# Exchanging row maxima by maximum operations, and moving the row sums of a slot behind its block of feed-forward work

## The chip, the cores and the metric

The kernel runs on one core of one Trainium2 chip. The metric is the device time of one execution in microseconds (us). The core has five engines that run their own instruction streams in order and meet through semaphores: TensorE (PE in the profile; PEld is its weight load), VectorE (DVE), ScalarE (ACT), GpSimd (POOL) and SyncE (SP, which here only issues transfers). SBUF is the on-chip memory with 128 partitions; PSUM is where TensorE writes.

## The reference

Attention with a threshold, then a gated feed-forward block. B = 8 batches, H = 8 heads, S = 576 rows of D = 64; the feed-forward block takes 4608 tokens of 512 through a width of 1536. All is float32.

```python
scale = 1.0 / np.sqrt(q.shape[-1])
scores = scale * np.matmul(q, k.transpose(0, 1, 3, 2))
thresh = np.max(scores, axis=-1, keepdims=True) - tau
scores = np.where(scores >= thresh, scores, -1000000000.0)
scores = scores - np.max(scores, axis=-1, keepdims=True)
attn = np.exp(scores)
attn = attn / (np.sum(attn, axis=-1, keepdims=True) + 1e-09)
attn_out = np.matmul(attn, v)
x = attn_out.transpose(0, 2, 1, 3).reshape(B * S, H * D)
g = x @ w_gate
silu = g * (1.0 / (1.0 + np.exp(-g)))
out = (silu * (x @ w_val)) @ w_out
```

For every row of scores, so, a maximum is needed before anything else, and a sum after the masking.

## The kernel before

Two heads are handled together: a segment is one pair of heads of one batch (32 pairs). A segment consists of tiles of 128 rows of queries; a slot is the work on one tile, and behind the scores of each slot come two portions of the feed-forward block of tokens that are already through attention. `fill(part)` emits such a portion. The first batch is handled tile by tile with whole rows in a lane (20 slots). From the second batch on, segments are *halved* (28 segments of 5 slots, 140 in all): a row of 576 scores lies half in one group of 32 partitions and half in the neighbouring group. So the maximum and the sum of a row are each made in two halves, and neighbouring groups must exchange them. The function `meet` does that: column 0 of a small tile holds a group's own half, and column 1 gets the neighbour's. Four copies do it, one for each group of 32 partitions.

```python
def meet(x, m, copy):
    for g in range(NG):                      # NG = 4 groups of G = 32 partitions
        o = g ^ 1
        copy(x[g * G:(g + 1) * G, 0:m, 1:2], x[o * G:(o + 1) * G, 0:m, 0:1])
```

The scores of one tile are a generator; the main loop advances it between portions of the block (m is 4 halves of rows per lane, 2 in the last tile of a segment):

```python
def scores(seg, t):
    # ... score tiles in PSUM (ps_s: 2 buffers of 2 banks; a full tile takes both) and their matmuls (L266) ...
    if halved:
        # ...
        for x, tile_ in enumerate(pss):
            nc.vector.tensor_reduce(out=mx[:, 2 * x:2 * x + 2, 0], in_=tile_[:, :, 0:SH],
                                    axis=AX.X, op=ALU.max, negate=True)               # L286
        meet(mx, m, nc.vector.tensor_copy)                                            # L244
        nc.vector.tensor_reduce(out=nm[:, 0:m], in_=mx[:, 0:m, :], axis=AX.X, op=ALU.min)   # L289
    # ... the case of whole rows ...
    if halved:
        nc.scalar.activation(th[:, 0:m], nm[:, 0:m], AF.Identity, bias=cut, scale=-1.0)     # L298
    for x in range(m):
        # ...
        nc.scalar.activation(ps[x], scs[x], AF.Exp, bias=nm[:, x:x + 1])              # L302
    yield                                                                             # 1
    turn(1)                                  # turns p of an earlier tile in 32x32 blocks (L334)
    for x in range(m):                       # masking, with the sum of each half row
        nc.vector.scalar_tensor_tensor(out=ps[x], in0=scs[x], scalar=th[:, x:x + 1], in1=ps[x],
                                       op0=ALU.is_ge, op1=ALU.mult, accum_out=sm[:, x, 0:1])   # L306
    tot = stp.tile([P, 4], F32, name="tot")
    if halved:
        meet(sm, m, nc.scalar.copy)                                                   # L244
        yield                                                                         # 2
        nc.vector.tensor_reduce(out=tot[:, 0:m], in_=sm[:, 0:m, :], axis=AX.X, op=ALU.add)  # L312
    # ... else: the sum alone ...
    nc.vector.reciprocal(out=ri[:, 0:m], in_=tot[:, 0:m])                             # L315
    if not halved:
        yield                                                                         # 2
    for x in range(m):
        if halved and not split:             # split: weights are still being joined
            nc.gpsimd.tensor_scalar(out=ps[x], in0=ps[x], scalar1=ri[:, x:x + 1], ...)      # L320
        else:
            nc.scalar.activation(ps[x], ps[x], AF.Copy, scale=ri[:, x:x + 1])         # L322
    # ... p goes on a list, to be turned two slots later ...
    yield                                                                             # 3
```

The block's part in a portion is a gate product (`pg`, 8 or 16 matmuls) that ScalarE copies out of PSUM, a value product (`pv`) that VectorE multiplies with it, or output matmuls (`po`):

```python
def gate(j, cs, f, hts, gts):
    # ...
    ps = rows_of_products(j, cs, f, 0, "pg")                                          # L443
    nc.scalar.copy(gts[f // per][:, f % per:f % per + GR, :], ps)                     # L457

def value(j, cs, f, hts, gts):
    # ...
    ps = rows_of_products(j, cs, f, 1, "pv")                                          # L443
    nc.vector.tensor_tensor(out=hts[f // 2][:, :, 0:n], in0=gts[...], in1=ps, op=ALU.mult)  # L463

def sigmoids():                              # once enough gates have gathered
    for _, gt, own in unsig:
        nc.scalar.activation(gt, gt, AF.Sigmoid)                                      # L472
        for x, ht in enumerate(own):
            nc.gpsimd.tensor_tensor(out=ht, in0=ht, in1=gt[:, 2 * x:2 * x + 2, :], op=ALU.mult)  # L474
```

The main loop, cut to the order of a slot:

```python
for n, seg in enumerate(segs):
    for x, t in enumerate(seg["tiles"]):
        go = scores(seg, t)
        next(go)                             # to yield 1
        # ... transposes and products of whole-row tiles, loads, a piece of weights split ...
        next(go)                             # to yield 2
        if more:
            join_weights()                   # 4 VectorE, 2 GpSimd operations, in the first stage only
        fill(part)                           # first part
        next(go)                             # to yield 3
        if len(unsig) >= SIG:
            sigmoids()
        fill(part)                           # second part
        if attends and n > 2 * NP:
            next(products)                   # p times v (xa, L401), copies to xall (L412, L420)
            next(products)
        # ... loads, and VectorE's transposes of the next segment's q and k ...
```

Of the kernel before, what the change touches and what calls it, by code (L numbers as in the profile page):

```python
# [13 lines left out]
ALU = mybir.AluOpType  # L14
AX = mybir.AxisListType
# [3 lines left out]
def kernel(  # L19
# [28 lines left out]
    nc = tc.nc  # L48
# [6 lines left out]
    G = 32  # L55
# [25 lines left out]
    op = ctx.enter_context(tc.tile_pool(name="op", bufs=1))  # L81
# [112 lines left out]
    def need(n):  # L194
        while len(joined) < n:
            fetch_weights(2)
            if not split:
                split_weights()
            join_weights()
            split_weights()  # L200
# [39 lines left out]
    def meet(x, m, copy):  # L240

        for g in range(NG):
            o = g ^ 1
            copy(x[g * G:(g + 1) * G, 0:m, 1:2], x[o * G:(o + 1) * G, 0:m, 0:1])  # L244

    def scores(seg, t):
        qT, kT, tiles, halved = seg["qT"], seg["kT"], seg["tiles"], seg["halved"]
        if halved and "p" not in seg:
            seg["p"] = ptp.tile([P, 2 * NT + 1, S], F32, name="p")
        q0 = t * P - seg["q0"]  # L250
        heads = [slice(h * D, (h + 1) * D) for h in range(2)]
        if t < NT:
            pss = [ps_s.tile([P, 2, 512], F32, name="sc") for _ in range(2)]
            at = [tiles.index(t), len(tiles) + tiles.index(t)]
        else:
            pss = [ps_s.tile([P, 2, 512], F32, name="sc")]
            at = [tiles.index(t)]
        if halved:
            put = [(pss[h], u, h, q0 + u * D) for u in range(2) for h in range(2)] if t < NT else \
                [(pss[0], h, h, q0) for h in range(2)]  # L260
            for x in range(0, len(put), 2):
                for g in range(NG):
                    a, c = divmod(g, 2)
                    for ps, u, h, col in put[x:x + 2]:
                        hs = heads[h]
                        nc.tensor.matmul(ps[g * G:(g + 1) * G, u, 0:SH], qT[hs, col + a * G:col + (a + 1) * G],  # L266
                                         kT[hs, c * SH:(c + 1) * SH], start=True, stop=True)
        elif t < NT:
            for h, hs in enumerate(heads):
                for n in range(2):  # L270
                    nc.tensor.matmul(pss[h][:, n, 0:SH], qT[hs, q0:q0 + P], kT[hs, n * SH:(n + 1) * SH],
                                     start=True, stop=True)
        else:
            for n, h in ((0, 0), (1, 1), (1, 0), (0, 1)):
                hs = heads[h]
                nc.tensor.matmul(pss[0][hs, n, 0:SH], qT[hs, q0:q0 + D], kT[hs, n * SH:(n + 1) * SH],
                                 start=True, stop=True)
        mx, nm, th, ri = (stp.tile([P, 4, 2] if x == "mx" else [P, 4], F32, name=x) for x in ("mx", "nm", "th", "ri"))
        sm = sums[0]
        sums.rotate(1)  # L280
        if halved:
            m = 2 * len(at)
            scs = [ps[:, u, 0:SH] for ps in pss for u in range(2)]
            ps = [seg["p"][:, x, u * SH:(u + 1) * SH] for x in at for u in range(2)]
            for x, tile_ in enumerate(pss):
                nc.vector.tensor_reduce(out=mx[:, 2 * x:2 * x + 2, 0], in_=tile_[:, :, 0:SH], axis=AX.X, op=ALU.max,  # L286
                                        negate=True)
            meet(mx, m, nc.vector.tensor_copy)
            nc.vector.tensor_reduce(out=nm[:, 0:m], in_=mx[:, 0:m, :], axis=AX.X, op=ALU.min)  # L289
        else:  # L290
            m = len(at)
            scs = [ps[:, :, 0:SH] for ps in pss]
            ps = [pbufs[0][:, x, :].rearrange("p (n s) -> p n s", n=2) for x in range(m)]
            pbufs.rotate(1)
            for x in range(m):
                nc.vector.tensor_reduce(out=nm[:, x:x + 1], in_=scs[x], axis=AX.XY, op=ALU.max, negate=True)
# [4 lines that stand above are left out]
                nc.scalar.activation(th[:, x:x + 1], nm[:, x:x + 1], AF.Identity, bias=cut, scale=-1.0)  # L301
            nc.scalar.activation(ps[x], scs[x], AF.Exp, bias=nm[:, x:x + 1])  # L302
        yield
        turn(1)
        for x in range(m):
            nc.vector.scalar_tensor_tensor(out=ps[x], in0=scs[x], scalar=th[:, x:x + 1], in1=ps[x],  # L306
                                           op0=ALU.is_ge, op1=ALU.mult, accum_out=sm[:, x, 0:1])
        tot = stp.tile([P, 4], F32, name="tot")
        if halved:
            meet(sm, m, nc.scalar.copy)  # L310
            yield
            nc.vector.tensor_reduce(out=tot[:, 0:m], in_=sm[:, 0:m, :], axis=AX.X, op=ALU.add)  # L312
        else:
            nc.vector.tensor_reduce(out=tot[:, 0:m], in_=sm[:, 0:m, 0:3:2], axis=AX.X, op=ALU.add)
        nc.vector.reciprocal(out=ri[:, 0:m], in_=tot[:, 0:m])  # L315
        if not halved:
            yield
        for x in range(m):
            if halved and not split:
                nc.gpsimd.tensor_scalar(out=ps[x], in0=ps[x], scalar1=ri[:, x:x + 1], scalar2=None, op0=ALU.mult)  # L320
# [3 lines that stand above are left out]
            unturned.append([seg["p"][:, x, :] for x in at])  # L324
        else:
            unflipped.append((seg, t, [p.rearrange("p n s -> p (n s)") for p in ps]))
        yield

    unturned = deque()

    def turn(keep):
        while len(unturned) > keep:
            for p in unturned.popleft():
                nc.vector.transpose(out=p, in_=p)  # L334
# [223 lines left out]
    def fill(n):  # L558

        credit[0] += n  # L560
        while credit[0] > 0:
            c = next(pieces)
            left[0] -= c
            credit[0] = credit[0] - c if c else 0
            if not c:
                return 0
        return 1
# [53 lines left out]
    def fetch_qk(i):  # L621
        if i < NPAIR and i not in raws and i not in kept:
            raws[i] = load_qk(i)
# [23 lines left out]
    def give(n):  # L647
        for u in segs[n]["gives"]:
            ready.append(u)
            left[0] += cost(u)  # L650
        gains[n] = (gains[n][0], 0)
# [9 lines left out]
    for n, seg in enumerate(segs):  # L661
        if NP <= n < 2 * NP:
            seg["v"] = segs[seg["i"]]["v"]
        for x, t in enumerate(seg["tiles"]):
            go = scores(seg, t)
            next(go)
            attends = prev is not None and x == 1
            products = iter(())
            attend_tile()
            flip()  # L670
            if n == NP and x == 0:
                attend_tile()
                give(n - 1)
            if n == 2 * NP and x == 1:
                give(n - 1)
            if attends and n > 2 * NP:
                if prev["i"] % NP == 0:
                    need(NCC * DFF // FW + DM // ne * DFF // FW)
                    start_batch(prev["i"] // NP)
                products = attend(prev)  # L680
            part = pace(n, x) / 2
            more = len(split)
            if n or x:
                split_weights()
                fetch_weights(2)
            if x == 0 and n >= NP:
                fetch_qk(seg["i"] + 1)
            next(go)
            if more:
                join_weights()  # L690
            fill(part)
            next(go)
            if len(unsig) >= SIG:
                sigmoids()
            fill(part)
            if attends and n > 2 * NP:
                next(products)
                next(products)
                give(n - 1)
            if attends and seg["halved"]:  # L700
                load_v(seg)
            if x == 0 and 0 < n < NP:
                load_v(seg)
            if x == len(seg["tiles"]) - 2 and n + 1 < len(segs):
                prepare(segs[n + 1])
                if n < NP:
                    fetch_qk(segs[n + 1]["i"] + 1)
        prev = seg
# [39 lines left out]
```

## Time and profile before

| what | value |
|---|---|
| time, median of 3 runs | 1701.67 us (1696.55 to 1704.74) |
| span of the profiled execution | 1702.9 us |
| mean granted TensorE clock | 0.97 |
| VectorE copies of maxima (L244) | 560, 189.8 us, 339 ns each |
| ScalarE copies of sums (L244) | 560, 108.5 us, 194 ns each |
| sum of halves (L312), reciprocal (L315) of full tiles | 112 each, 165 and 178 ns each |
| VectorE waiting for the copies of sums | 97.0 us, 130 times |

Times are in us unless marked ns. Line numbers such as L244 are those of the kernel before. A line of the groups or waits names line, engine, operation, and written and read tiles; "idle before ... <-" says what ended the time in which the engine stood before those instructions. In a timeline each line begins with start and length, and brackets hold the idle time before it and its releaser. A line of waits has the engine, its tile and line, what it waited for, the total, how many times, and the longest. In the slices of the span each digit is the busy share in tenths. A matmul's end is modelled, so a TensorE shown as busy is not always at its peak.

### The profile page before, as it was taken

How to read it: one execution, taken by the hardware profiler on the slowest of the kernel's cores; microseconds unless marked ns; L12 is line 12 of the kernel's file. 1: busy time of each engine (PE TensorE's matmuls, PEld its weight loads, DVE VectorE, ACT ScalarE, POOL GpSimd, SP SyncE). 2: the span in 40 equal slices, each digit the busy share in tenths (PEclk: the TensorE clock that was granted, in tenths of full speed). 3: DMA queues.
4: the chain of work that ended last, by engine and by line, in shares of the span. 5: the costliest groups of instructions: out<-in, count | busy, mean ns of one | idle time of the engine just before them, and what ended most of it. 6: DMA issues, size and time to landing. Idle time of an engine off the chain costs nothing.

```text
span 1702.9 us, 30134 instructions
## 1 busy us (share of the span) xinstructions
PE 1585.5 (93%) x11344; PEld 1048.8 (62%) x11344; DVE 1103.2 (65%) x3058; ACT 716.3 (42%) x1864; POOL 779.6 (46%) x726
## 2 busy tenths in 40 slices
PE   6898768889999999999999999999999999999998
PEld 4675445347665766557665666575745675677765
DVE  6877878777676767667776677766777777600000
ACT  5785654334444444444444344343535353411110
POOL 3454455445544545445544465454546354511211
PEclk9899889999999999999999999999999999999999
DMA  7441221111111110111111110111111110000000
GB/s 164 138 131 60 62 47 29 41 41 29 35 35 35 35 29 15 34 35 36 29 41 29 42 35 10 38 22 42 29 42 28 41 29 28 1 13 1 13 13 13
DMA packets 176417, 66.84 MB, mean 39 GB/s; under 512 B 159632, under 2 KB 159632, under 8 KB 176272
## 3 DMA queue, kind: packets, MB, share of 16 engines
q1 hardware_dynamic: 173328, 55.47, 14.4%
q0 software_dynamic: 2944, 9.44, 1.6%
q8 instruction: 90, 1.47, 0.4%
q14 instruction: 55, 0.45, 0.1%
HBM read 55.44 MB, written 9.44 MB: 38 GB/s over the span
## 4 chain that ended last, share of the span: by engine, by line
PE 66%; DVE 17%; ACT 5%; issue 2%; POOL 2%; DMA 0%; SPq 0%; DVEq 0%; POOLq 0%; ACTq 0%
PE pg L443 17%; PE po L489 17%; PE pv L443 17%; PE sc L266 8%; PE xa L401 7%; DVE mx L244 5%; DVE p L306 4%; DVE mx L286 3%; DVE p L334 2%; ACT L302 1%; ACT p L302 1%; POOL p L320 1%; ACT sums L244 1%; DVE nm L289 0%; DVE wo L185 0%
## 5 line engine op out<-in xcount | busy, mean ns | idle before, releaser
L320 POOL TENSOR_SCALAR p<-p,ri 128x288 f32<-128x288 f32 x486 | 479.2, 1001 | 545.5 <-DVE ri L315 483.1
L443 PE MATMUL pg<-xall,wgv 128*128 128x256 f32 (+1 forms) x1824 | 404.7, 375 | 5.7 <-POOL wgv L190 5.7
L443 PE MATMUL pv<-xall,wgv 128*128 128x256 f32 (+1 forms) x1824 | 405.7, 376 | 0.0
L443 PEld LDWEIGHTS pg<-xall,wgv 128*128 128x128 f32 x1824 | 332.6, 193 | 76.6 <-issue 14.6
L489 PE MATMUL po<-wo,ht 128*128 128x512 f32 x816 | 370.8, 607 | 9.1 <-POOL ht L474 9.1
L443 PEld LDWEIGHTS pv<-xall,wgv 128*128 128x128 f32 x1824 | 335.1, 194 | 63.1 <-issue 14.0
L306 DVE SCALAR_TENSOR_TENSOR p<-sc,th,p 128x288 f32<-128x288 f32 (+1 forms) x540 | 258.6, 530 | 57.5 <-ACT p L302 56.6
L489 PEld LDWEIGHTS po<-wo,ht 128*128 128x128 f32 x816 | 153.6, 193 | 205.4 <-issue 188.2
L266 PE MATMUL sc<-kT,qT 64*32 64x288 f32 x4032 | 189.4, 427 | 69.4 <-DVE p L306 68.8
L302 ACT ACTIVATE p<-sc,nm 128x288 f32<-128x288 f32 (+1 forms) x540 | 236.7, 511 | 0.7
L298 ACT ACTIVATE th<-nm,cut 128x4 f32<-128x4 f32 (+1 forms) x140 | 41.6, 297 | 458.5 <-DVE nm L289 458.4
L286 DVE TENSOR_REDUCE mx<-sc 128x2 f32<-128x576 f32 x252 | 179.4, 749 | 56.4 <-PE sc L266 55.4
L244 DVE COPY mx<-mx 32x4 f32<-32x4 f32 (+1 forms) x560 | 189.8, 339 | 10.5
L463 DVE TENSOR_TENSOR ht<-gt,pv 128x512 f32<-128x512 f32 (+1 forms) x108 | 70.8, 656 | 190.5 <-PE pv L443 174.0
L334 DVE STREAM_TRANSPOSE p<-p 128x576 f32<-128x576 f32 x252 | 181.4, 754 | 6.0 <-POOL p L320 6.0
L266 PEld LDWEIGHTS sc<-kT,qT 64*32 64x32 f32 x4032 | 71.7, 108 | 173.2 <-issue 144.8
L244 ACT COPY sums<-sums 32x4 f32<-32x4 f32 (+1 forms) x560 | 108.5, 194 | 165.5 <-DVE p L306 158.7
L474 POOL TENSOR_TENSOR ht<-ht,gt 128x512 f32<-128x512 f32 (+1 forms) x108 | 127.7, 1209 | 82.2 <-ACT gt L472 82.2
L401 PE MATMUL xa<-p,vall 64*64 64x288 f32 x2016 | 131.2, 409 | 6.4 <-issue 5.1
L401 PEld LDWEIGHTS xa<-p,vall 64*64 64x64 f32 x2016 | 80.7, 134 | 56.6 <-issue 11.1
L457 ACT COPY gt<-pg 128x512 f32<-128x512 f32 (+1 forms) x114 | 63.7, 561 | 104.4 <-PE pg L443 102.9
L312 DVE TENSOR_REDUCE tot<-sums 128x4 f32<-128x12 f32 (+1 forms) x140 | 23.0, 164 | 97.0 <-ACT sums L244 97.0
(78 smaller groups left out, 963.3 us busy)
## 6 DMA issues: line engine op xcount, KB each, us to landing
vall<-in_v_dram SPq DMA_DIRECT2D x112, 144.0 KB, 3.2
qraw<-in_q_dram SPq DMA_DIRECT2D x128, 72.0 KB, 2.3
kraw<-in_k_dram SPq DMA_DIRECT2D x128, 72.0 KB, 2.7
out_dram<-ob POOLq DMA_DIRECT2D x32, 256.0 KB, 2.4
wo<-in_moe_w_gate_dram SPq DMA_DIRECT2D x16, 384.0 KB, 3.5
wo<-in_moe_w_val_dram SPq DMA_DIRECT2D x16, 384.0 KB, 4.0
xall<-in_moe_w_out_dram SPq DMA_DIRECT2D x6, 768.0 KB, 4.7
wo<-in_moe_w_out_dram SPq DMA_DIRECT2D x2, 768.0 KB, 4.2
```

The lines of the kernel that those rows point to most:

```text
L244: copy(x[g * G:(g + 1) * G, 0:m, 1:2], x[o * G:(o + 1) * G, 0:m, 0:1])
L266: nc.tensor.matmul(ps[g * G:(g + 1) * G, u, 0:SH], qT[hs, col + a * G:col + (a + 1) * G], kT[hs, c * SH:(c + 1) * SH], start=True, stop=True)
L286: nc.vector.tensor_reduce(out=mx[:, 2 * x:2 * x + 2, 0], in_=tile_[:, :, 0:SH], axis=AX.X, op=ALU.max, negate=True)
L302: nc.scalar.activation(ps[x], scs[x], AF.Exp, bias=nm[:, x:x + 1])
L306: nc.vector.scalar_tensor_tensor(out=ps[x], in0=scs[x], scalar=th[:, x:x + 1], in1=ps[x], op0=ALU.is_ge, op1=ALU.mult, accum_out=sm[:, x, ...
L320: nc.gpsimd.tensor_scalar(out=ps[x], in0=ps[x], scalar1=ri[:, x:x + 1], scalar2=None, op0=ALU.mult)
L334: nc.vector.transpose(out=p, in_=p)
L401: nc.tensor.matmul(xa[a][h * D:(h + 1) * D, at:at + n * G].rearrange("d (i q) -> d i q", q=G), vr[rs, h, j, :], p[rs, lo:lo + n, j, :], st ...
L443: nc.tensor.matmul(ps[:, i], wgv[:, mat, c, (f + i) * P:(f + i + 1) * P], x[:, c, cs], start=(c == 0), stop=(c == NCC - 1))
L463: nc.vector.tensor_tensor(out=hts[f // 2][:, :, 0:n], in0=gts[f // per][:, f % per:f % per + GR, :], in1=ps, op=ALU.mult)
L474: nc.gpsimd.tensor_tensor(out=ht, in0=ht, in1=gt[:, 2 * x:2 * x + 2, :], op=ALU.mult)
L489: nc.tensor.matmul(po, hts[f // 2][:, f % 2, i * P:(i + 1) * P], wo[:, f, :], start=(f == 0), stop=(f == NF - 1))
```

## The change

The exchange of maxima is done by VectorE reductions with the operation maximum over an axis of one element, in place of copies; the result is the same number. The ScalarE copies of row sums move behind the slot's first part of the block, and the sum of the two halves, its reciprocal and the scaling of p move behind the second part. To that end the generator has one more yield, the main loop one more step, and a tile of whole rows one more (empty) yield. The purpose is to take away from VectorE what holds its copies, to let ScalarE serve the block before it stands for the masking, and to let VectorE meet finished copies of sums.

```diff
@@ meet
-            copy(x[g * G:(g + 1) * G, 0:m, 1:2], x[o * G:(o + 1) * G, 0:m, 0:1])
+            copy(out=x[g * G:(g + 1) * G, 0:m, 1], in_=x[o * G:(o + 1) * G, 0:m, 0:1])
+
+    def largest(out, in_):
+        nc.vector.tensor_reduce(out=out, in_=in_, axis=AX.X, op=ALU.max)
+
+    def same(out, in_):
+        nc.scalar.copy(out, in_[:, :, 0])
@@ scores
-            meet(mx, m, nc.vector.tensor_copy)
+            meet(mx, m, largest)
             nc.vector.tensor_reduce(out=nm[:, 0:m], in_=mx[:, 0:m, :], axis=AX.X, op=ALU.min)
@@
         tot = stp.tile([P, 4], F32, name="tot")
         if halved:
-            meet(sm, m, nc.scalar.copy)
+            yield
+            meet(sm, m, same)
             yield
             nc.vector.tensor_reduce(out=tot[:, 0:m], in_=sm[:, 0:m, :], axis=AX.X, op=ALU.add)
@@
             unflipped.append((seg, t, [p.rearrange("p n s -> p (n s)") for p in ps]))
+            yield
         yield
@@ main loop
             if len(unsig) >= SIG:
                 sigmoids()
             fill(part)
+            next(go)
             if attends and n > 2 * NP:
                 next(products)
```

## The prediction

> **What bounds the kernel now.** I read the page first, the engine shares and the 40 slices, to see whether one engine fills the span.
>
> ```profile
> PE 1585.5 (93%) x11344; PEld 1048.8 (62%) x11344; DVE 1103.2 (65%) x3058; ACT 716.3 (42%) x1864; POOL 779.6 (46%) x726
> ...
> PE   6898768889999999999999999999999999999998
> ```
>
> TensorE is busy for 1585.5 of 1702.9 us. All that a change outside TensorE can take away is the remaining 117 us, and what TensorE loses to a lower clock. The idle time lies mostly in the first nine slices (some 380 us). So next I cut the span by stage: 0 to 165 us is the attention of the first batch (not halved, no exchange of maxima), 165 to 400 is the halved attention while weights are still being joined, 400 to 1490 is the steady stage, and after that only the feed-forward tail is left. The columns are the stretch, its length, busy us of PE, weight load, DVE, ACT and POOL, then the granted clock, DMA share and GB/s.
>
> ```profile
> 0.00:165.00 165.00, 139.10 (x948) 96.18 (x948) 123.81 (x264) 115.53 (x211) 75.41 (x48) 0.94 0.46 126
> 165.00:400.00 235.00, 187.11 (x1420) 113.86 (x1417) 187.27 (x502) 101.58 (x286) 116.44 (x102) 0.91 0.19 42
> 400.00:1490.00 1090.00, 1053.77 (x8157) 691.63 (x8156) 778.14 (x2271) 473.23 (x1320) 557.99 (x547) 0.98 0.14 31
> 1490.00:1703.00 213.00, 205.53 (x826) 147.12 (x824) 14.03 (x23) 25.99 (x48) 29.75 (x30) 0.99 0.03 10
> ```
>
> The change touches only the halved stages. There TensorE stands idle 235 - 187 = 48 us in the first and 1090 - 1054 = 36 us in the second, 84 us in all. The waits of TensorE, asked for each of the two stretches, say what ended that idle time; the first line is 165 to 400, the other two are 400 to 1490.
>
> ```profile
> PE sc L266 <- DVE p L306: 42.6, 20, 5.2
> ```
> ```profile
> PE sc L266 <- DVE p L306: 26.2, 29, 2.8
> PE po L489 <- POOL ht L474: 9.1, 3, 4.0
> ```
>
> Nearly all of it is one wait. A slot is one tile of scores with two portions ("parts") of the feed-forward block behind it. The score matmuls of a slot fill all score banks, and those of the next slot need the banks that VectorE's masking (L306) has read to the end. So the loop that can hold TensorE is: scores, row maxima (L286), exchange of maxima between partition groups (L244), minimum (L289), Exp on ScalarE, masking, next scores. VectorE is the busier half of that loop: in 165 to 400 it works 187 us, exactly as long as TensorE.
>
> A timeline of one steady slot shows the two things the change attacks.
>
> ```profile
> 658.48 3.72 POOL L474 TENSOR_TENSOR ht<-ht,gt 128x512 f32<-128x512 f32 x3
> ...
> 659.32 1.42 DVE L286 TENSOR_REDUCE mx<-sc 128x2 f32<-128x576 f32 x2 [0.18 <-PE sc L266]
> 660.78 1.79 DVE L244 COPY mx<-mx 32x4 f32<-32x4 f32 x4
> ...
> 664.41 1.67 ACT L302 ACTIVATE p<-sc,nm 128x288 f32<-128x288 f32 x4
> ...
> 667.21 0.85 ACT L244 COPY sums<-sums 32x4 f32<-32x4 f32 x4 [1.13 <-DVE p L306]
> ...
> 668.08 0.59 ACT L457 COPY gt<-pg 128x512 f32<-128x512 f32 x1
> 668.09 0.17 DVE L312 TENSOR_REDUCE tot<-sums 128x4 f32<-128x12 f32 x1 [0.91 <-ACT sums L244]
> ...
> 668.70 0.69 DVE L463 TENSOR_TENSOR ht<-gt,pv 128x512 f32<-128x512 f32 x1 [0.23 <-ACT gt L457]
> ```
>
> First, four copies of four numbers per lane take 1.79 us, and they end about when GpSimd's operation ends (658.48 + 3.72 = 662.20). Second, ScalarE is through with Exp at 666.08, stands 1.13 us for the masking, and only after its four copies of row sums may it take the gate result (gt) out of PSUM; VectorE in turn stands 0.91 us for those copies and then 0.23 us for gt. The answer for the tile mx has the rest: minimum, median and maximum in ns.
>
> ```profile
> L244 DVE COPY mx<-mx x560: 156/172/1703, 167.5 to 1480.4; 32x4 f32<-32x4 f32 x150, 32x2 f32<-32x2 f32 x37
> ...
> L289 DVE TENSOR_REDUCE nm<-mx x140: 156/161/164, 170.2 to 1480.8; 128x4 f32<-128x8 f32 x112, 128x2 f32<-128x4 f32 x28
> ```
>
> The copy's minimum equals a small reduction's, but its maximum is ten times that; the reduction never strays from 156 to 164. The copy's mean in the groups is 339 ns (189.8 us over 560).
>
> **What the Trainium skill says.** Page "SBUF — State Buffer", section "Who interferes with whom": VectorE's second port pair is GpSimd's only one; a VectorE copy in a two-port mode and a GpSimd operation shut each other out for a whole instruction, while tensor_reduce on trn2 never contends. The two lines above agree (1703 against 164 ns at most). Page "VectorE: DVE Perf Modes", section "The perf-mode tier table (the rule you actually need)": an fp32 SBUF copy runs in a 2x mode, tensor_reduce only in 1x. For four elements per lane that lost rate can't matter: 156 against 156 ns at the minimum. Page "TensorE: Matmul & The Clock Gate", section "Part 1: The HAM clock gate (the "warmup" mystery)": after an idle window TensorE runs at half clock until it has been busy for a while. The trace agrees: the granted clock is 0.91 where TensorE is 80% busy and 0.98 where it is 97% busy. So a removed wait pays a little more than its own length.
>
> **The change part by part.** (1) Maxima. 560 VectorE copies become 560 reductions over an axis of one element, so a maximum of one number. By the row of L289 I give each 161 ns. In 165 to 400 there are 100 copies of 396 ns mean: 100 x (396 - 161) = 23.5 us less. In 400 to 1490 there are 460 of 326 ns: 460 x (326 - 161) = 76 us less. Together 99 us of VectorE, 0.7 us for each of the 140 slots, all of it inside the loop that TensorE can wait for. (2) Row sums. The four ScalarE copies (560 of 194 ns, unchanged in number) move from in front of a slot's first part to behind it. A gt copy in the first part no longer sits behind the wait for the masking and 0.85 us of copies. (3) Sum and reciprocal. The reduction (L312, 164 ns) and reciprocal (L315, 176 ns) and the scaling of p behind them on GpSimd move from the middle of a slot to its end. By then the copies are done, so VectorE's wait for them should mostly go: 16.1 us in 165 to 400, 80.8 us in 400 to 1490, 97 us in all; I expect some 10 us left. (4) The order of matmuls on TensorE is the same in both programs; the extra step for tiles that are not halved moves nothing.
>
> For the slot above by hand: the maxima take 4 x 0.17 = 0.68 for 1.79 us, so masking ends 1.1 us earlier, at 666.07. gt is copied at 664.98, at the end of Exp, so ht follows the masking at once and ends at 666.75; the sums are copied from 666.1 to 666.95, sum and reciprocal end at 667.33. The next maxima, which started at 669.31, could start at 667.35, if its scores are there. So a slot where VectorE is the bound gains about 1.4 us on average (0.7 + 0.7) and 2 us in this one.
>
> What of it reaches the end? In 165 to 400 VectorE works 187 us and waits 16 us for sums, so it is released by 23.5 + 15 = 38 us; TensorE's waits of 42.6 us (20 of them, 2.1 us each) can shrink by about 1.4 us each, 20 x 1.4 = 28 us. In 400 to 1490 the 29 waits are 0.9 us long on average, shorter than 1.4 us, so I take 22 of the 26.2 us as gone. Of the 9.1 us on GpSimd's ht I take 4, since gt and its sigmoid come earlier in GpSimd's order than the scaling now. Clock: 187 us of work at 0.91 and 1054 at 0.98 lose at most 0.09 x 187 = 17 and 0.02 x 1054 = 21 us; with two thirds of the waits gone I give back 6 + 6. Sum 28 + 22 + 4 + 12 = 66 us. Against it I set 6 us for waits that take their place: sum and reciprocal (0.34 us) now stand between a slot's last ht and the next maxima, and scaling ends later. Net 60 us: 1702 - 60 = 1642 us.
>
> **The rivals.** (a) TensorE is the bound already, and the freed VectorE time only turns into VectorE waiting for TensorE. For it: 97% busy in 400 to 1490, where 76 of the 99 us are saved. Against it: the 42.6 us in 165 to 400 are open waits. It would leave some 25 us of gain: 1677 us. (b) The late scaling becomes the new wait. A tile's p is scaled by GpSimd (4 x 1.0 us), turned by VectorE two slots later (L334) and then used. Half a slot of about 4.5 us later, and behind up to three products of 1.24 us, it would eat the slack. Now the turn waits for GpSimd only 6.0 us in the whole run, once, and GpSimd is 51% busy in the steady stage; a slot's reserve is about one slot. If it did bite in the 29 or so slots with a sigmoid at 1 us each, the result would be about 1670. (c) GpSimd was itself slowed by VectorE's copies, and the stage gets more back. The scaling is steady at 992 to 1017 ns, so I give it nothing. (d) All waits on masking go and the clock recovers to 1.0: 69 + 9 + 30 us, 1594 us; the other parts of the loop (Exp with its 1.28 us table load, turning, joining of weights) speak against it.
>
> **Range and chances.** The size hangs on how much of 69 us of waits a loop shortened by 1.4 us releases, and on the clock. Between a (1677) and most of d I put 1616 to 1670 for 8 in 10. The 2% line is at 1667.6 us. Faster by over 2%: 0.84; within 2%: 0.14; slower: 0.02, as nothing is added on any engine and the one new order with risk has slack.
>
> **What would show it.** Right: the exchange line as reductions of about 160 ns with a maximum near the median; the VectorE wait for sums near 10 us instead of 97; TensorE waiting for masking about 20 us instead of 69; the clock of 165 to 400 above 0.91. Wrong: reductions as ragged as the copies (then the port is not the cause); a new large wait of L334 on GpSimd, or of sum on ScalarE at the slot's end; TensorE's wait for masking unchanged, with the released VectorE time showing up as VectorE waiting for scores or products.

## The result, and the profile after

The changed kernel takes 1617.51 us (median of 4 runs, 1616.54 to 1618.6) against 1701.48 us (4 runs): a ratio of 0.951, 95% interval 0.9485 to 0.9533. That is 84 us less, where 60 us less was predicted; the time lies inside the predicted range, near its lower edge. In the changed kernel the exchange of maxima is L247, of sums L250, the scores L272, the maxima L292, the minimum L295, the masking L312, the sum L319, the scaling L327 and the turn L342.

The chain that ended last, by engine, on the page of the kernel before:

```profile
PE 66%; DVE 17%; ACT 5%; issue 2%; POOL 2%; DMA 0%; SPq 0%; DVEq 0%; POOLq 0%; ACTq 0%
```

The page of the changed kernel, with engine shares, TensorE's slices and the same chain:

```profile
PE 1546.1 (96%) x11344; PEld 1031.3 (64%) x11344; DVE 996.4 (62%) x3058; ACT 710.7 (44%) x1864; POOL 779.7 (48%) x726
...
PE   6898879899999999999999999999999999999998
...
PE 80%; DVE 7%; ACT 2%; issue 1%; POOL 1%; POOLq 0%; DVEq 0%; ACTq 0%
```

TensorE now carries 80% of the chain and VectorE 7%, where they carried 66% and 17%. TensorE's idle time fell from 117.4 to 1615.6 - 1546.1 = 69.5 us, by 48 us. But its busy time fell too, by 39 us, for the same 11344 matmuls.

To see where, both spans are cut at the same work: from the minimum of the 1st halved slot to that of the 26th, and on to that of the 140th. Columns as in the prediction. First the kernel before, then the changed one.

```profile
170.20:405.60 235.40, 187.98 (x1444) 114.45 (x1445) 186.21 (x504) 102.71 (x290) 116.51 (x103) 0.91 0.20 45
405.60:1480.80 1075.20, 1043.00 (x8097) 685.54 (x8096) 770.17 (x2251) 467.09 (x1304) 548.89 (x539) 0.99 0.14 31
```
```profile
166.80:376.00 209.20, 179.48 (x1447) 109.50 (x1446) 163.79 (x505) 102.21 (x290) 116.94 (x104) 0.94 0.22 51
376.00:1395.50 1019.50, 1015.64 (x8100) 674.86 (x8099) 687.21 (x2250) 462.01 (x1304) 549.69 (x539) 1.00 0.15 32
```

The first 25 slots gained 26 us and the 114 of the steady stage 56 us. In the steady stage TensorE is now busy for 1015.6 of 1019.5 us at a clock of 1.00: idle time went from 32 to 4 us, busy time from 1043 to 1016 us. In the first 25 slots 30 us of idle time are left.

TensorE's waits in the changed kernel, the first line for 164 to 370 us, the other two for 370 to 1403 us:

```profile
PE sc L272 <- DVE p L312: 23.4, 20, 3.7
```
```profile
PE sc L272 <- DVE p L312: 3.7, 3, 2.4
PE po L497 <- POOL ht L482: 1.0, 1, 1.0
```

The tile mx (ns: minimum, median, maximum):

```profile
L247 DVE TENSOR_REDUCE mx<-mx x560: 142/148/154, 166.1 to 1395.3; 32x4 f32<-32x4 f32 x150, 32x2 f32<-32x2 f32 x37
...
L295 DVE TENSOR_REDUCE nm<-mx x140: 156/160/163, 166.8 to 1395.5; 128x4 f32<-128x8 f32 x112, 128x2 f32<-128x4 f32 x28
```

No exchange operation takes more than 154 ns, where a copy had taken up to 1703. The busy time of the exchange fell from 189.8 to 83.2 us. Last, a timeline of a steady slot:

```profile
763.23 0.64 DVE L247 TENSOR_REDUCE mx<-mx 32x4 f32<-32x4 f32 x4
...
767.04 0.68 DVE L471 TENSOR_TENSOR ht<-gt,pv 128x512 f32<-128x512 f32 x1
767.16 0.81 ACT L250 COPY sums<-sums 32x4 f32<-32x4 f32 x4 [1.21 <-DVE p L312]
768.00 0.17 DVE L319 TENSOR_REDUCE tot<-sums 128x4 f32<-128x12 f32 x1 [0.28 <-ACT sums L250]
```

The exchange takes 0.64 us and ht follows the masking at once, but the sum still stands 0.28 us for ScalarE's copies. In the whole run this wait is 62.4 us (91 times), not the 10 us that were predicted. The end of a slot in program order is often no later in VectorE's time. The copies cannot start before the masking ends and take 0.81 us, while VectorE has at most little to do in between: in the trace 81 of the 140 slots have one ht of 0.68 us between masking and sum, and in 50 slots nothing stands there, as their parts of the block hold no value product. These 50 slots make 49 of the 62 us, about 1 us each; in the kernel before there were 95 such slots, with 86 of its 97 us.

### The profile page after: what moved, and what is told of

Same layout as the page of the kernel before. It is cut to its first block, busy times and chain, and to the rows that moved or that the text cites. A ratio compares the mean times of both kernels' runs of the same rounds, so it can differ in the third digit from the quotient of the medians.

```text
span 1615.6 us, 30135 instructions
## 1 busy us (share of the span) xinstructions
PE 1546.1 (96%) x11344; PEld 1031.3 (64%) x11344; DVE 996.4 (62%) x3058; ACT 710.7 (44%) x1864; POOL 779.7 (48%) x726
## 4 chain that ended last, share of the span: by engine, by line
PE 80%; DVE 7%; ACT 2%; issue 1%; POOL 1%; POOLq 0%; DVEq 0%; ACTq 0%
PE po L497 21%; PE pv L451 21%; PE pg L451 21%; PE sc L272 9%; PE xa L409 8%; DVE p L312 2%; DVE mx L292 1%; DVE p L342 1%; DVE mx L247 1%; POOL p L327 1%; ACT p L308 1%; DVE wo L185 0%; ACT L308 0%; DVE wo L183 0%; DVE wo L181 0%
## 5 line engine op out<-in xcount | busy, mean ns | idle before, releaser
L327 POOL TENSOR_SCALAR p<-p,ri 128x288 f32<-128x288 f32 x486 | 479.0, 1001 | 290.6 <-DVE ri L322 248.7
L451 PE MATMUL pv<-xall,wgv 128*128 128x256 f32 (+1 forms) x1824 | 398.8, 372 | 0.0
L451 PEld LDWEIGHTS pv<-xall,wgv 128*128 128x128 f32 x1824 | 330.2, 191 | 59.7 <-issue 13.6
L497 PE MATMUL po<-wo,ht 128*128 128x512 f32 x816 | 364.0, 598 | 1.0 <-POOL ht L482 1.0
L312 DVE SCALAR_TENSOR_TENSOR p<-sc,th,p 128x288 f32<-128x288 f32 (+1 forms) x540 | 258.5, 529 | 57.3 <-ACT p L308 56.4
L292 DVE TENSOR_REDUCE mx<-sc 128x2 f32<-128x576 f32 x252 | 179.3, 748 | 73.3 <-PE sc L272 69.9
L471 DVE TENSOR_TENSOR ht<-gt,pv 128x512 f32<-128x512 f32 (+1 forms) x108 | 70.8, 655 | 232.4 <-PE pv L451 227.4
L272 PE MATMUL sc<-kT,qT 64*32 64x288 f32 x4032 | 170.8, 413 | 27.3 <-DVE p L312 27.1
L342 DVE STREAM_TRANSPOSE p<-p 128x576 f32<-128x576 f32 x252 | 181.3, 753 | 2.2 <-POOL p L327 2.2
L250 ACT COPY sums<-sums 32x4 f32<-32x4 f32 (+1 forms) x560 | 108.5, 194 | 137.4 <-DVE p L312 130.0
L272 PEld LDWEIGHTS sc<-kT,qT 64*32 64x32 f32 x4032 | 66.5, 106 | 120.5 <-issue 93.3
L506 POOL DMA_DIRECT2D out_dram<-ob x32 | 19.3, 603 | 171.3 <-ACT ob L501 169.0
L247 DVE TENSOR_REDUCE mx<-mx 32x4 f32<-32x4 f32 (+1 forms) x560 | 83.2, 149 | 10.4
```

What stands on the lines that cost most here:

```text
L247: nc.vector.tensor_reduce(out=out, in_=in_, axis=AX.X, op=ALU.max)
L250: nc.scalar.copy(out, in_[:, :, 0])
L451: nc.tensor.matmul(ps[:, i], wgv[:, mat, c, (f + i) * P:(f + i + 1) * P], x[:, c, cs], start=(c == 0), stop=(c == NCC - 1))
L497: nc.tensor.matmul(po, hts[f // 2][:, f % 2, i * P:(i + 1) * P], wo[:, f, :], start=(f == 0), stop=(f == NF - 1))
```

## The experiments

All ratios are to the kernel before, run beside them; it took 1701.5 us beside the changed kernel and 1700.8, 1700.4 and 1699.7 us beside the later groups, so that two or three us between rows say little. Diffs are against the changed kernel unless said otherwise. A table of what was measured (waits and busy time in us, from each run's profile):

| run | time | ratio (95%) | VectorE busy | VectorE waits for sums | TensorE waits for masking (halved) | clock |
|---|---|---|---|---|---|---|
| before | 1701.5 | 1 | 1103.2 | 97.0 | 68.8 | 0.970 |
| changed | 1617.5 | 0.9485 to 0.9533 | 996.4 | 62.4 | 27.1 | 0.985 |
| maxima only | 1633.9 | 0.9580 to 0.9621 | 998.4 | 96.9 | 31.9 | 0.983 |
| order only | 1694.2 | 0.9950 to 0.9974 | 1120.2 | 64.4 | 70.8 | 0.977 |
| copies late, sum with them | 1629.0 | 0.9548 to 0.9595 | 997.8 | 105.3 | 30.5 | 0.983 |
| copies early, sum late | 1623.6 | 0.9523 to 0.9573 | 995.7 | 57.7 | 29.3 | 0.984 |
| maxima with two inputs | 1669.8 | 0.9810 to 0.9839 | 1074.3 | 64.3 | 60.4 | 0.977 |
| sums by reductions | 1621.2 | 0.9519 to 0.9548 | 1078.3 | none | 31.0 | 0.983 |
| exchange twice | 1665.5 | 0.9777 to 0.9807 | 1078.1 | 64.4 | 46.7 | 0.979 |
| exchange thrice | 1719.6 | 1.0093 to 1.0126 | 1161.5 | 65.0 | 81.6 | 0.973 |
| no exchange | 1602.5 | 0.9414 to 0.9443 | 913.5 | 61.7 | 20.4 | 0.988 |
| Exp table early | 1617.0 | 0.9502 to 0.9530 | 995.3 | 62.5 | 26.0 | 0.983 |
| turn split | 1621.3 | 0.9529 to 0.9561 | 1002.5 | 24.5 | 29.9 | 0.987 |
| table early, turn split | 1620.6 | 0.9521 to 0.9549 | 1005.1 | 24.4 | 26.6 | 0.982 |

**The two halves of the change, alone.** My theory was that both shorten one loop (scores, maxima, exchange, Exp, masking, next scores); the rivals were that one of them is everything.

```diff
# maxima only (against the kernel before)
-            meet(mx, m, nc.vector.tensor_copy)
+            meet(mx, m, largest)
```


> Maxima by reductions, sums where they were. Theory (both halves shorten one and the same loop, about 0.7 us per slot each, until TensorE has no more waits): VectorE loses about 100 us of busy time, its wait for the copies of sums stays near 97 us, TensorE's wait for masking falls from 69 to some 45 us, time 1650 to 1665. Rival A (the ragged copies were everything): 1617 to 1625. Rival B (the order was everything): 1690 to 1702.

```diff
# order only
-            meet(mx, m, largest)
+            meet(mx, m, copied)          # copied: nc.vector.tensor_copy of the same column
```


> Sums in the new order, maxima still by copies. Theory (two halves of one loop): 1645 to 1665, the wait for copies of sums falls from 97 to about 60 us. Rival A (the ragged copies were everything): 1690 to 1702, or slower, as the scaling on GpSimd now starts just ahead of the next exchange and holds its copies longer: mean of a copy above 339 ns. Rival B (the order was everything): 1617 to 1625.

The maxima alone bring 67 us, the order alone 6.5 us, both 84 us. The even split of my theory is wrong. Rival A is nearer: the order alone falls into its range, with its longer copies; the maxima alone (1633.9) lie between its 1625 and my 1650. One reason stands in the row of the exchange in the order-only kernel (busy us, mean ns, idle before):

```profile
L250 DVE COPY mx<-mx 32x4 f32<-32x4 f32 (+1 forms) x560 | 208.3, 372 | 10.5
```

With the scaling on GpSimd moved to the slot's end, just ahead of the next exchange, a copy takes 372 ns on average and not 339: 18.5 us more over 560. In the traces 468 of the copies now meet a running GpSimd operation, where 429 did. VectorE's wait for sums fell by 33 us, so the loop gained 15 us and the time 6.5. Behind reductions, which are not held, the same order is worth 1633.9 - 1617.5 = 16 us. The halves are not independent: the first makes the second worth having.

**The order, taken apart.**

```diff
# copies late, sum with them
             meet(sm, m, same)
-            yield
             nc.vector.tensor_reduce(out=tot[:, 0:m], ...)      # sum, reciprocal, scaling ahead of the second part
             # ... reciprocal, scaling ...
+            yield                                              # the step behind the second part stays, empty
```


> As the changed kernel, but sum, reciprocal and scaling follow directly on the late copies of sums, ahead of the second part. If the gain of the order lies in ScalarE serving the gate before it stands for the masking: within 5 us of 1617.5. If it lies in VectorE not standing for the copies: VectorE's wait for sums is back near 100 us and the time lies 20 to 35 us above the changed kernel's. My theory says both count: 1625 to 1640.

```diff
# copies early, sum late
-            yield
             meet(sm, m, same)
+            yield
             yield
```


> As the changed kernel, but the copies of sums stay in front of the slot's first part; sum, reciprocal and scaling at the slot's end. If VectorE not standing for the copies is what counts: within 5 us of 1617.5, with the wait for sums near 10 us. If ScalarE serving the gate first counts: 20 to 35 us above. My theory says both count: 1620 to 1640.

Starting from 1633.9 with neither: late copies alone bring 4.9 us, the late sum alone 10.3 us, both 16.4 us. Both seem to count and roughly add, as expected, but each is small: the ratio intervals overlap between neighbours, though the runs do not (1631.5 to 1634.3 with neither, 1625.1 to 1631.1 with late copies, 1623.4 to 1626.7 with the late sum, 1616.5 to 1618.6 with both). With the sum late, VectorE's wait for sums is 57.7 us; with it early, 105.3 us. That wait did not fall to the 10 us expected for a late sum. A late sum takes 39 us off it beside early copies and 43 us beside late ones, and 10 and 12 us of these reach the end.

**What holds a copy.** The prediction's account comes from the Trainium skill, page "SBUF — State Buffer", section "Who interferes with whom": copies in a two-port mode contend with GpSimd, and so do operations with two SBUF inputs against a GpSimd operation that reads SBUF; tensor_reduce on trn2 doesn't. If that is the cause, a maximum of two inputs is held like a copy, though it computes.

```diff
-        nc.vector.tensor_reduce(out=out, in_=in_, axis=AX.X, op=ALU.max)
+        nc.vector.tensor_tensor(out=out, in0=in_[:, :, 0], in1=in_[:, :, 0], op=ALU.max)
```


> As the changed kernel, but each maximum is taken of the column with itself by a two-input elementwise maximum. Theory[...]: durations as ragged as the copies', maximum over 1000 ns, mean 250 to 400 ns, time 1625 to 1650. Rival (a copy was the trouble, any arithmetic operation is free of it): all within 140 to 200 ns and 1615 to 1620 us.

```profile
L247 DVE TENSOR_TENSOR mx<-mx x560: 148/156/1712, 165.5 to 1449.9; 32x4 f32<-32x4 f32 x150, 32x2 f32<-32x2 f32 x37
```

The rival falls. A maximum with two inputs in SBUF takes 156 ns in the median and up to 1712, mean 289, like a copy; that it computes does not free it. The traces also show that GpSimd is what holds: in the kernel before, 131 of the 560 copies ran while GpSimd did nothing, and none of these took over 166 ns, while all 254 copies of over 300 ns overlap a GpSimd operation. With two inputs it is the same (86 beside an idle GpSimd, at most 160 ns; all 131 of over 300 ns overlap one). Of the changed kernel's reductions 462 overlap a GpSimd operation and none takes more than 154 ns. This agrees with the page; which port an operation reads through is not seen in a trace. The time was above what I had given it (1669.8 for 1625 to 1650), as the loop weighs more than I thought; the next runs measure that.

**How much a loop's length weighs.** The exchange is repeated with the same result, or left out.

```diff
-            meet(mx, m, largest)
+            for _ in range(2):           # or 3
+                meet(mx, m, largest)
```


> As the changed kernel, with the exchange of maxima done twice (same result): 4 more reductions, about 0.6 us per slot in the loop, 90 us of VectorE in all. If the loop no longer holds TensorE in the steady stage: 1617.5 plus 15 to 30 us (the stage of joining weights and some clock). If the loop were still the bound everywhere: plus 80 us or more.

> As the changed kernel, with the exchange of maxima done three times: 1.25 us per slot in the loop, about the length the copies and the wait for sums had. Theory (the length of the loop, whatever fills it, sets TensorE's waits): TensorE's wait for masking about 60 us and the clock near 0.97 again, time 1670 to 1710, and most of it falls in the second dose, since the first one uses slack up. Rival (the copies hurt through GpSimd, not through the loop's length): below 1645.

```diff
# the exchange of maxima is left out: each half row uses its own maximum, the output is another
-            meet(mx, m, largest)
-            nc.vector.tensor_reduce(out=nm[:, 0:m], in_=mx[:, 0:m, :], axis=AX.X, op=ALU.min)
+            nc.vector.tensor_reduce(out=nm[:, 0:m], in_=mx[:, 0:m, 0:1], axis=AX.X, op=ALU.min)
```


> As the changed kernel, but the exchange of maxima is left out (each half row is masked and scaled by its own maximum, so the output is another); four reductions less per slot, 83 us of VectorE less. Adding them a second and third time cost 48 and 54 us. If the time follows the loop's length at the same rate below the changed kernel too: 1565 to 1575. If the changed kernel stands at the knee (in its steady stage TensorE is already busy throughout, only the stage of joining weights still waits): 1592 to 1607.

Each dose is 560 reductions, about 83 us of VectorE. Added once it costs 47.9 us, a second time 54.1 us; taken away it brings only 15.1 us. Per us of VectorE in the loop: 0.59, 0.65, and 0.18 below the changed kernel. The first dose lies between the two ranges I had given it (15 to 30 us, or 80 and more), and the second ends above its range (1719.6 us for 1670 to 1710, TensorE's wait for masking 81.6 us for about 60). So my guess that the first dose would use up slack was wrong: the changed kernel has next to none. It stands at the knee: where the loop gets longer TensorE waits at once, where it gets shorter nearly nothing is left. Here are the waits with three exchanges:

```profile
PE sc L272 <- DVE p L313: 81.6, 81, 4.4
...
DVE mx L292 <- PE sc L272: 29.7, 76, 2.6
```

and here with none:

```profile
DVE mx L292 <- PE sc L272: 104.6, 89, 5.5
...
PE sc L272 <- DVE p L311: 20.4, 24, 3.2
```

One wait replaces the other: with three, scores wait for masking (81.6 us); with none, the maxima wait for scores (104.6 us), that is, VectorE for TensorE. With three exchanges no operation of the exchange is held by GpSimd (142 to 155 ns each), and still the time is 1719.6 us, above the kernel before. So length alone, with nothing held, is enough. The copies cost no more than that: from the changed kernel to the one with its order and copies it is 76.7 us for 123.8 us of VectorE, 0.62 per us, between the 0.59 and 0.65 of the doses.

**Sums by reductions too.**

```diff
-            meet(sm, m, same)
+            meet(sm, m, largest)
```


> As the changed kernel, but the sums too are exchanged by VectorE reductions, four more of 148 ns per slot, and ScalarE copies none. Theory (TensorE is the bound from about 370 us on and has slack of VectorE there; before that VectorE is the bound): ScalarE loses 108 us of copies and 130 us of standing, VectorE gains 83 us of work and loses 62 us of standing; time within 8 us of 1617.5, lower if the gate served without delay counts. Rival (VectorE is still the bound throughout): 1630 or more.

1620.48 to 1621.7 us, 3.7 us above the changed kernel. VectorE works 82 us more and its wait for sums of 62 us is gone; ScalarE is freed of all copies, and the time does not fall. VectorE's wait was mostly time it could have filled with work, not time lost.

**Two attempts to get below.** The first loads the table for Exp at the end of a slot with sigmoids; the second lets the masking start before the second turn.

```diff
             next(go)
+            if loaded:                   # loaded: this slot had sigmoids
+                nc.scalar.activation(warm, cut, AF.Exp, scale=0.0)
```


> As the changed kernel, but after a slot with sigmoids ScalarE runs an Exp of one element per lane at the slot's end, so that the table for Exp is loaded (1.28 us, 29 times) before the next slot's maxima are ready and not between them and its Exp. If these loads hold the loop: VectorE's wait for Exp falls from 56 to about 20 us and the time by 5 to 20 us, 1598 to 1612. If they lie beside other work or only move the delay to the gate's copy: 1613 to 1620.

```diff
-        turn(1)
+        late = turn(1)                   # turns the first of the two, returns the second
         # ... masking ...
+        for p in late:
+            nc.vector.transpose(out=p, in_=p)
```


> As the changed kernel, but only one of the two turns of an earlier tile stands between the maxima and the masking, the other behind the masking. The masking then ends some 0.4 us earlier in slots where Exp is ready, VectorE's work stays the same. If the stretch from scores to the end of the masking is what TensorE waits for: 1600 to 1612. If VectorE's total work per slot is (the second turn then delays the next maxima just as long): 1613 to 1625.

> The last two together. If each shortens the loop where the other doesn't: the sum of both gains, 1590 to 1605. If the early table load gains nothing, the result of the split turn alone within 4 us.

```profile
DVE p L313 <- ACT p L309: 27.8, 42, 2.9
```

That line is from the kernel with the early table: VectorE's wait for Exp fell from 56.4 to 27.8 us as hoped, and the time stayed (1616.09 to 1617.6). The split turn made this wait 114.7 us, as the turn no longer fills it, cut the wait for sums to 24.5 us, and cost 3.8 us; both together gave 1620.6. TensorE's wait for masking stayed at 26.0 to 29.9 us in all three, where the changed kernel has 27.1. The early table fits the run without the exchange: at the knee, a shorter path brings next to nothing. The split turn tells less, as the masking then mostly stood for Exp instead of for the turn. None of these versions beats the changed kernel by more than the runs scatter.

## Why the prediction was right or wrong

- *The wait that bounds the kernel* (scores wait for masking, VectorE is the busier half of the loop): right. The doses move this wait from 20 to 82 us, and the time with it. The number 1617.5 lies only 1.5 us above the lower end of the range, as the gain was 84 and not 60 us.
- *Maxima*: 99 us of VectorE less was predicted, 106.6 measured. The reason, that GpSimd holds the copies and not a reduction, was right: the reduction is the only one of three operations that is never held, and the long copies are those that overlap GpSimd.
- *Wait for sums, 97 to 10 us*: wrong, 62 us. The prediction took the end of a slot for half a slot later in time. In VectorE's order the sum now has one ht of 0.68 us before it in 81 slots, and nothing in 50. The slot that the prediction worked out by hand already had a wait, 0.2 us between the end of ht (666.75) and that of the copies (666.95), which over 140 slots is 28 us and not 10. The miss cost little, as the run with sums by reductions shows. The two halves were valued as equals (0.7 and 0.7 us per slot); alone they are worth 67 and 6.5 us.
- *TensorE's waits*: 28 + 22 + 4 - 6 = 48 us of idle time was predicted, 48 measured. This agreement is partly luck: within it the first stage gave 18 us of idle time where 28 was predicted, and the steady stage 28 where 22 + 4 was, before the 6 us taken off.
- *What was mis-sized is the clock term of 12 us*, as the last 39 us came out of TensorE's busy time. In the traces the granted clock is 1.0 but for short stretches, nearly all of 3.4 or 6.8 us, in which it is 0.5. They add up to 103.3 us in the kernel before and to 48.0 us in the changed one, and TensorE is shown busy in 91.3 and 39.2 us of them. Gate and value matmuls follow each other every 216 ns at the full clock and every 427 ns in these stretches, so about half of that busy time is lost. By this estimate the loss fell from 46 to 20 us: 26 us come from the clock, not 12. In the steady stage 8 stretches of 30.7 us became none, so its whole loss of some 15 us went, of which I had given back 6; in the first 25 slots the loss fell from 20 to 10 us. The other 13 us I had not in the sum at all. Most of them are in the scores, whose rows (busy us, mean ns, idle before) are, before and changed:

```profile
L266 PE MATMUL sc<-kT,qT 64*32 64x288 f32 x4032 | 189.4, 427 | 69.4 <-DVE p L306 68.8
```
```profile
L272 PE MATMUL sc<-kT,qT 64*32 64x288 f32 x4032 | 170.8, 413 | 27.3 <-DVE p L312 27.1
```

18.6 us of busy time are gone for the same 4032 matmuls. By the same estimate the clock accounts for 9.0 of them (busy in stretches of half clock: 23.8 us before, 5.8 us changed). The rest is in good part waiting that the page counts as busy. The timeline of the kernel before has both forms of a slot's scores, whole and broken in two by the wait for masking:

```profile
658.03 1.20 PE L266 MATMUL sc<-kT,qT 64*32 64x288 f32 x32
...
666.45 0.64 PE L266 MATMUL sc<-kT,qT 64*32 64x288 f32 x2
...
667.33 1.20 PE L266 MATMUL sc<-kT,qT 64*32 64x288 f32 x30 [0.23 <-DVE p L306]
```

Whole, 32 matmuls are shown busy for 1.20 us; broken, for 0.64 + 1.20 = 1.84 us, with the idle time besides. Of the 112 full tiles 26 were broken before (TensorE idle between two of their matmuls) and 13 in the changed kernel; 13 x 0.64 = 8.3 us is most of the 9.6 us that the clock leaves. My sentence that a change outside TensorE can take away only its idle time and what it loses to its clock was wrong by this. What remains of the 13 us, some 5 us, is not accounted for.

- *The stages*: the first 25 slots were to gain 34 us by my terms and gained 26; the steady stage was to gain 32 and gained 56. I had capped its gain with TensorE's 26.2 us of shown waits.
- *Rival a* (TensorE is the bound already, 1677): wrong for the kernel before, right for the changed one, as the run without the exchange shows. *Rival b* (late scaling delays the turn): the turn waits 2.2 us for GpSimd in the changed kernel, so it didn't come; late scaling did cost something where copies were kept, as the order alone shows (372 ns a copy). *Rival c* (the copies slow GpSimd): a scaling takes 1001 ns on average in both kernels, so there was nothing to get back. *Rival d* (1594): the clock and waits of the steady stage did go; what is left is in the stage in which weights are joined, with 23.4 us of waits and a clock of 0.94, and in the first batch, which the change does not touch (clock 0.94).

A sizing that would have been better is only seen now: VectorE's loop lost 106.8 us of busy time and 34.6 us of waiting for sums, and 84 / 141.4 = 0.59 of it reached the end, the same share as with the exchange twice (0.59) and near that of the maxima alone (67 / 104.8 = 0.64). It was found after the result and not tested on a case of its own.

## What to carry to other kernels

Where two engines alternate in a loop and one of them is shown as busy nearly all the time (TensorE 97% in the steady stage here), its shown idle time is not the limit of the gain: waits that break a row of matmuls in two and a lower clock belong to it (here 48 us of idle time went, and 39 us of busy time with it). A dose experiment (the suspected step twice, thrice, not at all) measures the rate, and on which side of the knee the kernel stands. Where small copies in a loop show ragged durations beside a busy GpSimd (here 156 to 1703 ns), an operation that isn't held can take their place, such as a reduction over one element (142 to 154 ns). Moving a wait later in program order helps only as much as there is work of that engine in between.

## What the runs showed of the hardware

A maximum of a four-element column with itself by a two-input VectorE operation was held beside GpSimd like a copy: up to 1712 ns for a median of 156, and its mean of 289 ns is most of the copy's 339. Beside an idle GpSimd neither took more than 166 ns. A reduction over one element took 142 to 155 ns in all runs, a little less than the copy at its best (156). A row of 32 score matmuls that a wait broke in two was shown busy for 1.84 us and not 1.20. And the granted clock was halved in short stretches, 103 us in all before and 48 us changed. Over the runs its mean tended to be lower where TensorE had more idle time, 0.970 at 117 us (before), 0.979 at 91 (exchange twice), 0.985 at 69.5 (changed), but not strictly: 0.977 at 114 (order only), 0.973 at 127 (exchange thrice).
